# Filling empty expert slots row by row, one load for two heads' queries, and accumulating writes of one expert without dependence, in a fused attention and expert kernel

## The chip, the cores and the metric

One core of a Trainium2 chip runs the whole program. The metric is the device time of one launch in microseconds (us), the median of the runs. The engines are PE (TensorE, matrix products; its weight loads are counted apart as PEld), DVE (VectorE), ACT (ScalarE), POOL (GpSimd) and SP (SyncE), which does no arithmetic here and issues transfers. A "q" behind an engine's name (SPq, POOLq) is its sequencer, which issues transfers and waits. The core's transfers run on 16 DMA engines.

## The reference

Three layers follow each other.

1. Attention with a bucket mask, for 2 batches, 8 heads, 768 positions and a head width of 64. Each query and key gets six sign bits from a projection; a query sees only keys with the same bits. Softmax over the scaled scores, then the product with `v`.
2. A dense layer on the 1536 tokens of width 512: `h = x @ w_in` (512 to 2048), `g = h * sigmoid(1.702 h)`, `g @ w_out` (back to 512).
3. A mixture of 8 experts. Noisy gate logits pick two experts for each token:

```python
for e in range(E):
    for k in range(2):
        mask = top2[:, k] == e
        h = np.maximum(x[mask] @ w1[e], 0.0)
        out[mask] += top2_w[mask, k, None] * (h @ w2[e])
```

The operands of the products are split into a high and a low float16 half, and three products of halves replace one exact product.

## The kernel before

**Steps.** The work of layers 1 and 2 is laid out over numbered steps. A step `g` from 0 to 95 is one tile of 128 queries of one head against its 768 keys (`qk` L245, `rowmax` L258, `expo` L264, `e_hi` L301, `e_lo` L312 or, for the first 16, `e_turn` L278). Four such tiles (two heads by two tiles) make a unit, four units a chunk of 256 tokens, and there are six chunks. Some steps after a chunk's attention its dense layer follows in 16 pieces (`moe_pe` L446), then its routing (`route` L566). Tables in `PARAM` (L55, L56) say at which step each load, split and transpose stands.

**Order on the engines.** The program names each operation in the order of these steps. Up to step 99 a planner that comes with the language, which follows a modelled timeline, decides the order on each engine and its queue; from step 100 on (`GM=100`, L56, L950) the order is the one written out. The expert layer lies wholly in the written part.

**Loads.** All plain loads go through SP's queue. `load` (L115) fetches the queries of one unit in two transfers, one for each head of the pair (L120), into one tile `x`, and keys and values in one transfer for each head (L124). `stack_hi` (L128) and `stack_lo` (L151) split them; `stack_lo` also issues the first transpose of the stacked rows (L167, also on SP's queue), whose result `buckets` (L169) multiplies on PE (L177) to get the sign bits. `one_hot` and `stack_end` follow, with the second transpose (L209); then `qk` can use the unit. In the steps from 16 on the exponentials are also transposed by SP's queue (L323, tile `et`).

**Slots.** Tokens reach their experts through a table in DRAM, `slots`: rows of 1032 16-bit words (`ROW`, L30), of which 1024 are the token's two halves and 8 are token number, expert and weights. Expert `e` owns the 432 rows from `e * 432`. Not all are taken, so all 3456 are first filled by `init_slots` (L546), in seven calls at the steps 16, 18, ... 28. A call fills 512 rows (the last one 384): for each group of 128 rows one transfer writes the first 1024 words from a tile of zeros, 256 words at a time (L550), then one transfer writes the last 8 words of all groups from the tile `blank` (L552), where a row of its own behind the real output, `N + lane`, stands as the token number. The tiles `zeros`, `blank` and `blank2` are set on POOL at the start (L518 to L527). `init_out` (L554) fills the output with zeros, from the same tile `zeros`.

**Routing.** `r_t` (L561) transposes a tile of 128 tokens into a tile `xrt`, which has two buffers (the pool's default); `route` computes gate and position, and scatters the rows into `slots` with indirect transfers on POOL (L679). Before each one stands a memset of a one-element tile, `spacer` (L678), and the scatters are declared to have no dependence on each other (L683).

**Experts.** For each expert, `l1` (L785) and `l2` (L806) are the two products on PE. `l2` makes tiles 0 to 2 of 128 rows and a tile 3 of the last 48 rows, which is laid out as two halves of 256 columns. `l2_out` (L822) scales the tile on ACT (L828) and adds it to the output in DRAM with an accumulating indirect transfer on POOL (L830). All these adds go to one tensor with rows known at run time only, so each waits until the one before it has landed. Expert 0 is cut into two parts of two tiles each; the others have one part. The last expert's tile 3 is the last work of the program; behind it stands only a test whether any expert has over 432 tokens (L1033, L1034), which is false here.

Of the kernel before, what the change touches and what calls it, by code (L numbers as in the profile page):

```python
# [9 lines left out]
I32 = mybir.dt.int32  # L10
U32 = mybir.dt.uint32
I64 = mybir.dt.int64
U16 = mybir.dt.uint16
# [4 lines left out]
B, H, S, D = 2, 8, 768, 64  # L18
DM = H * D
N = B * S  # L20
# [9 lines left out]
ROW = 2 * DM + 8  # L30
NT = S // 128
HP = H // 2
CT = 2
# [21 lines left out]
PARAM = dict(GM=16, HE=lambda nm, b: 'D', OE=lambda nm, b: 'D', SC=lambda nm, b: 'D', WB=0, XO=lambda b: 'D', NG=16, WS=lambda i: 'P', TS=lambda g: True, XL=lambda g: 'D', GW=2, E0=7, T0=12, T1=16, EL=8, WX=3, PV={(1,2,3):4}, PVD=5, ST={}, VA={}, RA={}, O0=48, OS=2, IS=2, FU=16, VF=2, EC=lambda g: 'AA', QX=8, QS=3, EA=1, S1=(8,8,8,9,9,9,11,13), QE=8, XG=2, XB=2, PC=2, OH=3, BK=3, R0=18, R1=0, LK=8, WL=1, NW=3, LE=lambda nc: nc.scalar, I0=24, LQ=8, LV=0, W=[(g, 1) for g in range(-6, 30)], KA={(0,0,0):-8,(0,0,1):-6,(0,1,0):-4,(0,1,1):-2}, QA={(0,0,0):-7,(0,0,1):-3}, HI=lambda g: 'P', LO=lambda g: False)  # L55
# [4 lines left out]
def fused(ctx: ExitStack, tc: tile.TileContext, q, k, v, proj, w_in, w_out, w_gate, w_noise, noise,  # L60
          w1, w2, out, dbg=None):
    nc = tc.nc
    consts = ctx.enter_context(tc.tile_pool(name="consts", bufs=1))
    wts = ctx.enter_context(tc.tile_pool(name="wts", bufs=4))
    rt = ctx.enter_context(tc.tile_pool(name="rt", bufs=2))
# [14 lines left out]
                            channel_multiplier=1)  # L80
# [34 lines left out]
    def load(nm, b, u):  # L115
        hp, i = u
        if nm == "q":
            x = att.tile([128, 2, CT, D], F32, name="q32")
            for h in range(2):
                PARAM['LE'](nc).dma_start(x[:, h], q[b, 2 * hp + h].rearrange(  # L120
                    "(p c) d -> p c d", c=NT)[:, i * CT:(i + 1) * CT])
        else:
            x = att.tile([128, 1, NT, D], F32, name=f"{nm}32", tag="x32", bufs=4)
            PARAM['LE'](nc).dma_start(x[:, 0].rearrange("p c d -> p (c d)"), (k if nm == "k" else v)[b, 2 * hp + i].rearrange(  # L124
                "(p c) d -> p (c d)", c=NT))
        raw[nm, b, u] = x
# [366 lines left out]
    def moe_split(ci, i):  # L493
        if i < 8:
            th = mst.pop((ci, "th", i))
            if i % 2 == 0:
# [11 lines left out]
                            channel_multiplier=-1)  # L508
# [8 lines left out]
    nc.gpsimd.iota(tok, pattern=[[S, B], [1, NT]], base=0, channel_multiplier=NT)  # L517
    zeros = consts.tile([128, 256], U16)  # L518
    nc.gpsimd.memset(zeros, 0)
    blank = consts.tile([128, ROW - 2 * DM], U16)  # L520
    nc.gpsimd.memset(blank, 0)
    nc.gpsimd.iota(blank[:, :2].bitcast(I32), pattern=[[1, 1]], base=N, channel_multiplier=1)
    blank2 = consts.tile([128, ROW - 2 * DM], U16)
    nc.gpsimd.memset(blank2, 0)
    for h in range(2):
        nc.gpsimd.iota(blank2[h * 64:h * 64 + 64, :2].bitcast(I32), pattern=[[1, 1]], base=N + 128,
                       channel_multiplier=1)  # L527
# [16 lines left out]
    slots = dram.tile([E * N, ROW], U16)  # L544

    def init_slots(i):  # L546
        sl = slots[i * 512:min(i * 512 + 512, E * CAP)].rearrange("(k p) c -> p k c", p=128)
        n = sl.shape[1]
        for k_ in range(n):
            nc.sync.dma_start(sl[:, k_, :2 * DM].rearrange("p (u c) -> p u c", c=256),  # L550
                              zeros[:, None, :].to_broadcast([128, 2 * DM // 256, 256]))
        nc.sync.dma_start(sl[:, :, 2 * DM:], blank[:, None, :].to_broadcast([128, n, ROW - 2 * DM]))  # L552

    def init_out(i):  # L554
        n = min(NO - i * 128, 128)
# [156 lines left out]
    spacer = consts.tile([1, 1], F32)  # L712


    ew, eblk, xg, met, hts, yst = {}, {}, {}, {}, {}, {}

    def w12_load(e, i):
        x = m2.tile([128, 1024], F32, name="w32", bufs=4)
        eblk[e, i] = x
        if i < 4:  # L720
            nc.sync.dma_start(x, w1[e, i * 128:(i + 1) * 128, :])
        else:
            f = (i - 4) * 256
            nc.sync.dma_start(x.rearrange("p (a d) -> p a d", a=2),
                              w2[e, f:f + 256, :].rearrange("(a p) d -> p a d", p=128))
# [13 lines left out]
    def parts(e):  # L739
        return ((0, REG), (REG, CAP)) if e < EA else ((0, CAP),)  # L740
# [81 lines left out]
    def l2_out(e, p, t):  # L822
        wv, ti = met[e, p]
        o = t - parts(e)[p][0] // 128
        py = yst.pop((e, "y", t))
        nd = DM if t < NF else 256
        yo = m2.tile([128, DM], F32, name="yo", bufs=4)
        nc.scalar.activation(yo[:, :nd], py[:, :nd], AF.Copy, scale=wv[:, 0, o:o + 1])  # L828
        dst = out if t < NF else out.rearrange("n (a d) -> (n a) d", a=2)
        nc.gpsimd.indirect_dma_start(  # L830
            out=dst, out_offset=bass.IndirectOffsetOnAxis(ap=ti[:, o:o + 1], axis=0),
            in_=yo[:, :nd], in_offset=None, compute_op=OP.add)


    todo, first, early = {}, {}, {}
# [31 lines left out]
    def stacks(g, nm, b, u):  # L867
        oh = PARAM["OH"]
        at(g - 2, load, nm, b, u)
        at(g, stack_hi, nm, b, u)  # L870
        soon(g + 1, stack_lo, nm, b, u)
        start(g + PARAM['BK'], buckets, nm, b, u)
        at(g + oh, one_hot, nm, b, u)
        soon(g + oh + 1, stack_end, nm, b, u)

    for b in range(B):
        for hp in range(HP):
            g = b * NCH * 16 + 4 * hp
            for h in range(2):
                stacks(PARAM["KA"].get((b, hp, h), g - LK + 2 * h), "k", b, (hp, h))  # L880
                gv = next(x for x in range(g, NU, 16) if x >= FU) - PARAM["VA"].get((b, hp, h), LV - h)
                at(gv - 3, load, "v", b, (hp, h))
                soon(gv, v_hi, b, (hp, h))
                at(gv, v_lo, b, (hp, h))
            for cc in range(NCH):
                if g + 16 * cc < FU:
                    at(max(g + 16 * cc - PARAM["VF"], -2), v_load32, cc, hp)
        for cc in range(NCH):
            for hp in range(HP):
                g = (b * NCH + cc) * 16 + 4 * hp  # L890
                stacks(PARAM["QA"].get((b, cc, hp), g - LQ), "q", b, (hp, cc))
                gp = g + PARAM["PV"].get((b, cc, hp), PARAM["PVD"] if b * NCH + cc else 4)
                at(g + 3, norm, b, cc, hp)
                at(gp, pv, b, cc, hp)
                soon(gp + 1, pv_scale, b, cc, hp)
                at(gp + 1, pv_norm, b, cc, hp)
                at(gp + 2, pv_out, b, cc, hp)
# [17 lines left out]
    for i in range(-(-E * CAP // 512)):  # L915
        at(PARAM["I0"] + PARAM["IS"] * i, init_slots, i)
# [82 lines left out]
    for e in range(1, E):  # L999
# [5 lines left out]
        for i in range(8):  # L1005
            x = b0 + (b1 - b0) * i // 8 if e >= EA + 1 else PARAM["S1"][i]
# [11 lines left out]
    for x in range(-4, len(seq) + 2):  # L1018
        for _ in range(PARAM["QX"]):
            if x >= PARAM["QS"]:  # L1020
                next(gen, None)
        if 0 <= x - 1 < len(seq):
            k_, *a = seq[x - 1]
            (l1_out if k_ == "1" else l2_out)(*a)
        if 0 <= x < len(seq):
            k_, *a = seq[x]
            (l1 if k_ == "1" else l2)(*a)
        by_turns(todo.pop(x, []))
# [5 lines left out]
    with tc.If(most > CAP):  # L1034
        with tc.tile_pool(name="ov", bufs=1) as ov:
# [10 lines left out]
            x = ov.tile([128, 1024], F32)  # L1046
            wt = [wts.tile([128, 2, 4096], F16, name=f"wo{i}", tag="w") for i in range(2)]
            nc.vector.memset(cur, 0.0)
            with tc.For_i(0, E, 1) as e:
# [5 lines left out]
                with tc.If(here > CAP):  # L1055
                    for j, (src, sw) in enumerate(((w1, SW1), (w2, SW2))):
                        for i in range(4):
# [6 lines left out]
                            sl = slice(i * 1024, i * 1024 + 1024)  # L1064
# [76 lines left out]
```

## Time and profile before

| | us |
|---|---|
| runs | 850.34, 852.13, 854.86 |
| median | 852.13 |
| the profiled execution: its own time | 851.51 |
| the profiled execution: its span | 849.4 |

The profile shows one execution. Its span begins and ends with the first and the last record, and its own time is 2.1 us longer. Views used here: the page (busy time of each engine, and the span in 40 slices); the table by stretches; the timeline of an engine or queue, where the bracket behind a row tells how long the engine had been idle and what ended that; the list of waits (an engine and line, what released it, total, times, longest); the sums of one line; and the chain that ended last, in order of time. Rows of one kind may be merged, with their number behind an x.

### The profile page before, as it was taken

To read this page: it belongs to the slowest core of one execution; us is meant where nothing else is said; L and a number is where in the kernel's file an instruction comes from. 1 tells how busy PE (TensorE), PEld (TensorE's weight loads), DVE (VectorE), ACT (ScalarE), POOL (GpSimd) and SP (SyncE) were. 2 spreads that over 40 slices of the span, in tenths; PEclk is the share of its full clock that TensorE was granted. 3 is DMA by queue.
4 is the path that set the end of the run, shared out by engine and by line. 5 is a ranking of instruction groups with operands and counts; after the bars stand their busy time and mean duration, and the time that the engine had idled before them with its cause. 6 is when DMAs were issued, how large, how long until landed. Compare 5 with 4: busy or idle time off the path is not lost. (4 is left out here: it accounts for less than half of the span.)

```text
span 849.4 us, 14814 instructions
## 1 busy us (share of the span) xinstructions
PE 734.0 (86%) x5398; PEld 447.3 (53%) x5399; DVE 541.0 (64%) x1327; ACT 443.5 (52%) x859; POOL 270.9 (32%) x272
## 2 busy tenths in 40 slices
PE   1577658878988989798999999879999999999994
PEld 1354336435754665475567585556455554545542
DVE  8998679987896888568778527444543625335110
ACT  3777657657766686467467335244443434425210
POOL 6355437743334154214312143041021121211212
PEclk9988979998999999989999999989999999999997
DMA  8999998998999999976777634587865757766212
GB/s 205 227 253 230 210 223 179 220 212 173 179 155 214 161 190 194 223 134 106 149 131 122 139 108 122 177 200 167 221 145 168 209 120 194 156 172 162 38 15 36
DMA packets 285453, 141.03 MB, mean 166 GB/s; under 512 B 231552, under 2 KB 264384, under 8 KB 285376
## 3 DMA queue, kind: packets, MB, share of 16 engines
q1 hardware_dynamic: 278848, 126.37, 68.4%
q0 software_dynamic: 6528, 13.68, 9.2%
q8 instruction: 43, 0.70, 0.4%
q14 instruction: 34, 0.28, 0.1%
HBM read 61.49 MB, written 24.25 MB: 101 GB/s over the span
## 5 line engine op out<-in xcount | busy, mean ns | idle before, releaser
L792 PE MATMUL ph<-xg,ew 128*128 128x432 f16 (+2 forms) x864 | 146.8, 334 | 8.7 <-DMA xg<-slots 8.7
L456 PE MATMUL h<-xt,wi 128*128 128x256 f16 x1152 | 139.8, 276 | 2.0 <-DVE th L486 1.7
L467 PE MATMUL px<-wo,gt 128*128 128x512 f16 x576 | 134.9, 388 | 7.2 <-ACT wo L441 3.9
L736 DVE SCALAR_TENSOR_TENSOR ew<-w,ew 128x1024 f16<-128x1024 f32 x64 | 78.0, 1228 | 89.9 <-ACT ew L735 89.9
L830 POOL DMA_INDIRECT out_dram<-yo,ti x32 | 51.9, 1621 | 232.4 <-ACT yo L828 163.1
L814 PE MATMUL py<-ew,ht 128*128 128x512 f16 x576 | 125.8, 379 | 0.0
L456 PEld LDWEIGHTS <-wi 128*128 128x128 f16 x1152 | 112.1, 99 | 24.8 <-issue 5.5
L792 PEld LDWEIGHTS <-ew 128*128 128x128 f16 x864 | 85.3, 101 | 68.3 <-issue 6.4
L252 PE MATMUL s<-kt,qt 128*128 128x512 f16 (+1 forms) x384 | 90.6, 362 | 18.6 <-ACT e L271 14.6
L271 ACT ACTIVATE e<-s,mx 128x768 f32<-128x768 f32 x96 | 85.7, 894 | 34.0 <-DVE mx L262 19.7
L501 POOL TENSOR_TENSOR gt<-th,gt 128x512 f16<-128x512 f32 x48 | 60.2, 1254 | 114.9 <-ACT gt L500 111.3
L467 PEld LDWEIGHTS <-gt 128*128 128x128 f16 x576 | 55.9, 99 | 73.7 <-issue 10.6
L261 DVE TENSOR_REDUCE mx<-s 128x1 f32<-128x768 f32 x96 | 90.7, 949 | 6.3 <-PE s L252 6.1
L814 PEld LDWEIGHTS <-ht 128*128 128x128 f16 x576 | 56.3, 98 | 67.2
L319 DVE SCALAR_TENSOR_TENSOR er<-e,mx,er 128x768 f16<-128x768 f32 x68 | 71.2, 1049 | 24.3 <-ACT er L310 22.6
L310 ACT ACTIVATE er<-e,mx 128x768 f16<-128x768 f32 x68 | 63.3, 934 | 38.1 <-DMA et<-er 24.2
L802 ACT ACTIVATE ht<-ph 128x432 f16<-128x432 f32 (+2 forms) x72 | 35.3, 490 | 82.2 <-PE ph L792 82.2
L803 DVE SCALAR_TENSOR_TENSOR ht<-ph,ht 128x432 f16<-128x432 f32 (+2 forms) x72 | 40.0, 556 | 55.3 <-ACT ht L802 54.6
L828 ACT ACTIVATE yo<-py,wv 128x512 f32<-128x512 f32 (+1 forms) x32 | 20.3, 633 | 103.3 <-PE py L814 54.7
L735 ACT ACTIVATE ew<-w 128x1024 f16<-128x1024 f32 x64 | 66.3, 1047 | 2.5 <-DMA w<-in_moe_w_dram 2.5
L364 PE MATMUL pv<-et,vt 128*64 128x256 f16 x720 | 53.8, 283 | 13.9 <-DMA et<-er 13.9
L252 PEld LDWEIGHTS <-qt 128*128 128x128 f16 x384 | 37.1, 104 | 49.0 <-issue 26.5
(192 smaller groups left out, 930.0 us busy)
## 6 DMA issues: line engine op xcount, KB each, us to landing
w<-in_moe_w_dram SPq DMA_DIRECT2D x64, 512.0 KB
wraw<-in_moe_w_in_dram SPq DMA_DIRECT2D x16, 512.0 KB
wraw<-in_moe_w_out_dram SPq DMA_DIRECT2D x16, 512.0 KB
slots<-zeros SPq DMA_DIRECT2D x27, 256.0 KB
v<-in_v_dram SPq DMA_DIRECT2D x24, 192.0 KB
out_dram<-zeros SPq DMA_DIRECT2D x13, 256.0 KB
k<-in_k_dram SPq DMA_DIRECT2D x16, 192.0 KB
q<-in_q_dram SPq DMA_DIRECT2D x48, 64.0 KB
```

The costliest lines, as they stand in the source:

```text
L252: nc.tensor.matmul(ps[:, n0 * 128:n1 * 128], qt[:, s, h, t, :], kt[:, s, h, n0:n1, :].rearrange("p c t -> p (c t)"), start=(s == 0), stop= ...
L261: nc.vector.reduce_max(mx[:, 0:1], st[g]["ps"][:, :S], axis=AX.X)
L271: nc.scalar.activation(e32, st[g]["ps"][:, :S], AF.Exp, scale=0.125, bias=st[g]["mx"][:, 1:2], accum_out=sms[b, cc, hp][:, 2 * h + t:2 * h ...
L310: nc.scalar.activation(er[:, 0], st[g]["e"], AF.Copy, scale=r)
L319: nc.vector.scalar_tensor_tensor(er[:, 1], d["e"], d["mx"][:, 3:4], er[:, 0], op0=OP.mult, op1=OP.subtract)
L456: nc.tensor.matmul(ph[:, a, :], wi[ws][:, d, f0:f0 + 128], xt[:, d, xs, :], start=(d == 0 and ws == 0 and xs == 0), stop=(d == HP - 1 and ...
L467: nc.tensor.matmul(px, gts[ci, f // 2][:, gs, f % 2, t * 128:t * 128 + 128], wo[ws][:, f, :], start=(f == 0 and gs == 0 and ws == 0), stop ...
L501: nc.gpsimd.tensor_tensor(gt[:, 1], th, gt[:, 0], op=OP.subtract)
L735: nc.scalar.activation(hi, x, AF.Copy, scale=SW1 if j == 0 else SW2)
L736: nc.vector.scalar_tensor_tensor(lo, x, SW1 if j == 0 else SW2, hi, op0=OP.mult, op1=OP.subtract)
L792: nc.tensor.matmul(ph[:, :c1 - c0], w[:, ws, d * FE + f * 128:d * FE + f * 128 + 128], xg[e, p][:, xs * HP + d, :], start=(d == 0 and ws = ...
L814: nc.tensor.matmul(py, ht[:, f, hs, t * 128:t * 128 + 128], w[:, ws, f * DM:(f + 1) * DM], start=(i == 0), stop=(i == n - 1))
```

## The change

Three edits. `load` fetches the queries of both heads of a unit in one transfer; the pieces stay 512 bytes long (128 float32). `init_slots` fills its 512 rows in one transfer, with whole rows of 1032 words, from a tile `blank` that is now 1032 words wide and is taken from the buffers of `xrt`; `xrt` so becomes 16 bytes wider in each partition, and one of its two buffers holds `blank` until the last fill has read it. `l2_out` declares that the adds of one expert carry no dependence on each other (those of different experts still do), and puts a memset of `spacer` before each.

```diff
@@ load
             x = att.tile([128, 2, CT, D], F32, name="q32")
-            for h in range(2):
-                PARAM['LE'](nc).dma_start(x[:, h], q[b, 2 * hp + h].rearrange(
-                    "(p c) d -> p c d", c=NT)[:, i * CT:(i + 1) * CT])
+            PARAM['LE'](nc).dma_start(x.rearrange("p h c d -> p h (c d)"), q[b, 2 * hp:2 * hp + 2].rearrange(
+                "h (p c) d -> p h (c d)", c=NT)[:, :, i * CT * D:(i + 1) * CT * D])
@@ constants
-    blank = consts.tile([128, ROW - 2 * DM], U16)
+
+    blank = rt.tile([128, ROW], U16, name="blank", tag="xrt")
     nc.gpsimd.memset(blank, 0)
-    nc.gpsimd.iota(blank[:, :2].bitcast(I32), pattern=[[1, 1]], base=N, channel_multiplier=1)
+    nc.gpsimd.iota(blank[:, 2 * DM:2 * DM + 2].bitcast(I32), pattern=[[1, 1]], base=N, channel_multiplier=1)
@@ init_slots
         sl = slots[i * 512:min(i * 512 + 512, E * CAP)].rearrange("(k p) c -> p k c", p=128)
-        n = sl.shape[1]
-        for k_ in range(n):
-            nc.sync.dma_start(sl[:, k_, :2 * DM].rearrange("p (u c) -> p u c", c=256),
-                              zeros[:, None, :].to_broadcast([128, 2 * DM // 256, 256]))
-        nc.sync.dma_start(sl[:, :, 2 * DM:], blank[:, None, :].to_broadcast([128, n, ROW - 2 * DM]))
+        nc.sync.dma_start(sl, blank[:, None, :].to_broadcast([128, sl.shape[1], ROW]))
@@ l2_out
+    adds = {}
...
-        nc.gpsimd.indirect_dma_start(
+        nc.gpsimd.memset(spacer, 0.0)
+        ins = nc.gpsimd.indirect_dma_start(
             out=dst, out_offset=bass.IndirectOffsetOnAxis(ap=ti[:, o:o + 1], axis=0),
             in_=yo[:, :nd], in_offset=None, compute_op=OP.add)
+        for o_ in adds.setdefault(e, []):
+            tc.declare_no_dep(ins.ins, o_.ins, reason="a token is in an expert's slots once")
+        adds[e].append(ins)
```

## Rows read from the trace of the kernel before

**Rows 1.** The table by stretches: core, us, busy time and instructions of each engine.

```profile
core 0: us, PE busy (x) PEld busy (x) DVE busy (x) ACT busy (x) POOL busy (x), PEclk, DMA share, GB/s
60.00:112.00 52.00, 33.63 (x244) 19.81 (x243) 39.55 (x86) 36.73 (x86) 24.07 (x21) 0.87 1.17 225
112.00:200.00 88.00, 69.29 (x507) 42.23 (x507) 80.51 (x151) 59.28 (x115) 46.94 (x39) 0.91 1.00 206
340.00:480.00 140.00, 129.78 (x1049) 84.84 (x1049) 103.34 (x288) 82.41 (x164) 34.60 (x32) 0.96 0.77 142
540.00:818.00 278.00, 272.89 (x1715) 151.87 (x1714) 119.42 (x240) 106.12 (x161) 51.65 (x35) 0.98 0.64 157
```

**Rows 2.** The chain that ended last, its end: start us, us, what.

```profile
818.37 10.37 PE py L814 x48
...
828.82 0.70 ACT yo L828
829.52 0.66 issue
830.18 4.86 DMA out_dram<-yo,ti
...
835.79 4.90 DMA out_dram<-yo,ti
```

**Rows 3.** The end on POOL and ACT, two timelines: start us, us, engine, line, operation.

```profile
835.79 1.55 POOL L830 DMA_INDIRECT out_dram<-yo,ti  x1 [4.06 <-DMA out_dram<-yo,ti]
841.47 1.55 POOL L830 DMA_INDIRECT out_dram<-yo,ti  x1 [4.13 <-DMA out_dram<-yo,ti]
...
834.00 0.69 ACT L828 ACTIVATE yo<-py,wv 128x512 f32<-128x512 f32 x1 [4.49 <-PE py L814]
836.75 0.47 ACT L828 ACTIVATE yo<-py,wv 128x256 f32<-128x256 f32 x1 [2.06 <-PEq L1034]
```

**Rows 4.** Waits of PE between 60 and 125 us: total us, times, longest.

```profile
PE pb L177 <- DMA qt<-qsa: 10.3, 3, 4.8
PE pv L364 <- DMA et<-er: 3.6, 1, 3.6
```

**Rows 5.** Timeline of SP's queue around the longest wait for a query transpose.

```profile
96.46 4.44 SPq L550 DMA_DIRECT2D slots<-zeros  x3
100.94 0.55 SPq L552 DMA_DIRECT2D slots<-blank  x1
101.66 2.41 SPq L167 DMA_TRANSPOSE qt<-qsa  x1
```

**Rows 6.** Timeline of PE, the product after the longest of these waits.

```profile
109.97 0.19 PE L177 MATMUL pb<-pq,qt 128*128 128x12 f16 x1 [4.79 <-DMA qt<-qsa]
```

**Rows 7.** Timeline of POOL, scatters declared free of each other, with their spacers.

```profile
527.38 1.13 POOL L679 DMA_INDIRECT slots<-xr,si  x1 [0.21 <-issue]
528.51 0.09 POOL L678 MEMSET spacer<- 1x1 f32 x1
528.82 1.39 POOL L679 DMA_INDIRECT slots<-xr,si  x1 [0.21 <-issue]
```

**Rows 8.** The sums of L830: from issue to landing of the 32 adds.

```profile
DMA to landing us min/median/max: 3.9/5.3/7.4
```

**Rows 9.** Sums of lines on SP's queue (ns min/median/max, first, last); x19: before 112 us.

```profile
L550 SPq DMA_DIRECT2D slots<-zeros x27: 372/527/1847, 60.4 to 183.1; - x27
L550 SPq DMA_DIRECT2D slots<-zeros x19: 372/527/1847, 60.4 to 110.6; - x19
L552 SPq DMA_DIRECT2D slots<-blank x7: 373/554/1185, 75.9 to 184.1; - x7
L120 SPq DMA_DIRECT2D q<-in_q_dram x48: 358/430/1722, 1.3 to 393.2; - x48
```

**Rows 10.** The table by stretches: fills of 512-byte pieces (first three), then larger loads.

```profile
60.00:62.00 2.00, 2.00 (x29) 1.30 (x29) 2.00 (x10) 1.79 (x4) 0.00 (x0) 1.00 1.01 332
62.00:64.00 2.00, 2.00 (x21) 1.28 (x16) 2.00 (x7) 2.00 (x7) 1.95 (x2) 1.00 0.98 265
64.00:66.00 2.00, 2.00 (x15) 1.30 (x14) 2.00 (x5) 1.90 (x5) 1.51 (x1) 1.00 1.17 308
486.00:488.00 2.00, 2.00 (x13) 0.93 (x11) 0.49 (x4) 0.18 (x1) 0.00 (x0) 1.00 1.02 408
488.00:490.00 2.00, 2.00 (x12) 0.98 (x10) 0.73 (x5) 0.00 (x0) 0.89 (x1) 1.00 1.04 420
```

**Rows 11.** Timeline of POOL at the start of the program.

```profile
2.21 0.30 POOL L519 MEMSET zeros<- 128x256 uint16 x1
2.46 0.09 POOL L521 MEMSET blank<- 128x8 uint16 x1
3.86 0.92 POOL L143 TENSOR_TENSOR k<-k,ks 128x384 f32<-128x384 f32 x1 [0.48 <-DVE ks L142]
```

**Rows 12.** Timeline of SP's queue, transposes of `r_t` into the two buffers of `xrt`.

```profile
203.79 1.26 SPq L564 DMA_TRANSPOSE xrt<-xr  x1
211.15 1.63 SPq L564 DMA_TRANSPOSE xrt<-xr  x1
```

## The prediction

> **What bounds the kernel now.** I read the table by stretches first, since the program has stages with different limits. In the expert layer PE is busy 272.89 of 278 us [rows 1]: no transfer, and no instruction on POOL, sets the time there. In the stretch from 60 to 112 us nothing is full except the transfers: PE is busy 33.63 of 52 us, DVE 39.55, ACT 36.73, while the DMA share is 1.17 [rows 1]. From 112 to 200 us DVE is busy 80.51 of 88 us. From 340 to 480 us PE is busy 129.78 of 140 us. So a shorter transfer can buy time between 60 and 112 us, less after that, and nothing between 540 and 818 us.
>
> Then I read the end of the chain that ended last. Up to 828.8 us it is PE. After that come tile 1's activation, its add, and the whole of tile 2's add, 4.86 and 4.90 us, one behind the other [rows 2]. The two timelines say why: ACT has tile 3 ready at 836.75 + 0.47 = 837.22 us, but POOL issues its add at 841.47 us, released by a landing transfer [rows 3]. The last add waits 4.2 us for nothing but the order of the adds.
>
> Last I looked at what PE waits for between 60 and 125 us: three waits, 10.3 us in all, for the first transposes of queries, and one of 3.6 us for an `et` transpose [rows 4]. Ahead of the longest, 4.79 us up to 109.97 [rows 6], SP's queue spent 4.44 + 0.55 us on issuing slot fills [rows 5].
>
> Sums are made against the profiled execution's own time of 851.51 us. The median shown is 852.13 us, so 0.6 us is added at the end. A run-to-run difference of 0.5%, 4.3 us, is about what a measurement of this kernel can tell from no change.
>
> **The adds.** Removed is the wait of tile 3's add for tile 2's landing. Tile 2's add loses its wait too: its activation ends at 834.00 + 0.69 = 834.69, and between activation and issue lies 0.66 us where nothing else held it [rows 2], so it goes at about 835.35 instead of 835.79. POOL is then held for 1.55 us [rows 3], to 836.9, and a spacer and its gap take 0.09 + 0.21 us [rows 7], to 837.2. Tile 3 is ready at 837.22; with the 0.66 us it goes at 837.88, or, if the gap is only the scatters' 0.21 us, at 837.43. That is 3.6 to 4.0 us before 841.47. I take 3.7. What follows the last issue stays, unless two adds in flight slow each other: adds land 3.9 to 7.4 us after issue, median 5.3 [rows 8], and the two that stood alone took 4.9 [rows 2]. If the last one takes the median instead, 0.4 is lost; if it takes the longest, 2.5. So the edit is worth between 1.1 and 4.0 us. In front of the end the same edit moves adds of tiles 3 earlier, off PE's path. The 32 spacers cost 32 x 0.3 us spread over an engine that is busy 51.65 of 278 us [rows 1]; what hides them is PE's stretch for each tile, and without that cover only the last one would stand in the path, 0.3 us.
>
> **The fills, as instructions.** 27 + 7 issues become 7. At the medians, SP's queue spends 27 x 0.527 + 7 x 0.554 = 18.1 us on them and will spend 7 x 0.554 = 3.9 us if an issue costs what it did, or 7 x 1.847 = 12.9 us if a transfer four times as large is issued like the longest now [rows 9]. So 5 to 14 us of issuing go, between 60 and 185 us. I take the median, 14, as an issue shows no reason to grow.
>
> **The fills, as bytes.** The zeros are 27 x 128 x 2048 B = 7.08 MB. In the 6 us in which they lead, the DMA engines move 332, 265 and 308 GB/s, 302 on average; in a stretch of larger loads, 408 and 420 GB/s [rows 10]. Whole rows of 2064 B lie between the two. At 302 GB/s the fill holds the DMA engines for 23.4 us, at 414 for 17.1: a gain between 0 and 6.3 us, of which 19 of 27 transfers [rows 9], 4.4 us, fall before 112 us. The writes of the last 8 words vanish into the rows. I take 4 us in all.
>
> A rule speaks against this part. The Trainium skill, "DMA: Bandwidth & Descriptors", section "Specifications", puts the smallest transfer at line rate at 512 B, which the zeros already have; by it the bytes would take as long as before, and the sum would be some 2 us higher, 847.5. This trace disagrees as far as it goes: 302 against 414 GB/s, though with fills and loads in opposite directions.
>
> **The queries.** 24 of 48 issues go, 24 x 0.43 = 10.3 us of SP's queue between 1 and 393 us [rows 9]. Pieces and bytes stay, and the split waited for both heads before. By itself I cost it at nothing: where SP waits for data, a shorter issue gives only a longer wait. It helps between 60 and 112 us, and is in the next estimate.
>
> **What reaches the end of attention.** PE's 10.3 us of waits for query transposes [rows 4] are the part of the stretch that queue time can give back. Below nothing it cannot be shown to go (a rival has that); above it are 10.3 us. The relief before 112 us, 19/27 of the 4 us of bytes, 2.8, and most of the issuing, is nearer to half of the stall than to either end, so I take 5 of 10.3. After 112 us DVE is nearly full and `et` transposes begin, and some of an early start is waited away; I let 3.2 of the 5 us arrive at 480 us. That share is a choice, with bounds 0 and 1.
>
> **The wider blank.** A memset of 256 words takes 0.30 us and one of 8 words 0.09 [rows 11], so 1032 words take about 0.09 + 1024 x 0.21 / 248 = 0.96 us, 0.87 more. POOL idles 0.48 us before its first subtraction of keys [rows 11]; beyond that, 0.4 us falls on the start. If the planner sets it later it costs nothing; at most 0.9. I take 0.4. The borrowed buffer is free in time: the last fill is issued at 184.1 us [rows 9] and the transpose that needs the buffer comes second, at 211.15 us [rows 12].
>
> **Sum.** 851.51 - 3.7 - 3.2 + 0.4 = 845.0, and with 0.6 for the median 845.6 us; I say 845.5.
>
> **The rivals.**
>
> *The front is given back.* DVE's and PE's full stretches after 112 us [rows 1] take up what the fills free; only the adds count: 852.1 - 3.7 = 848.4 us, from 847 to 851. For it speaks that PE is at 93% from 340 to 480 us; against it, that DVE has 7.5 us to spare from 112 to 200 us, PE 18.7. Chance 0.27. The rule above would put the bytes' share of the front here.
>
> *The front gives more.* All 10.3 us return, with the 3.6 us wait of the first `et` transpose [rows 4], and arrive: 852.1 - 3.7 - 13.9 = 834.5 us. For it speaks that PE, DVE and ACT all idle in that stretch. Chance 0.14.
>
> *Slower: the big fill stands before a transpose.* A fill is now one block of 1.06 MB, 3.5 us at 302 GB/s, and nothing can be put between its parts as the planner does now. Where a block lands just ahead of a query transpose, PE waits as at 109.97, 4.8 us [rows 5, 6]. Seven such places cost 7 x 4.8 = 33.6 us in place of 10.3, 23.3 more, and with the adds' gain 872 us at the worst; half of them 3.5 x 4.8 - 10.3 = 6.5 more, and 855 us; five 13.7 more, and 862 us. Against it: today's parts already stand three and four together. It decides from four of seven on. Chance 0.14, at about 860.
>
> *The adds still wait.* If the declared freedom doesn't reach the waits, the end stays and only the front counts: 849.3 us. Against it, the scatters with the same declaration are issued 1.44 us apart, and what ended the idle time between them was no transfer [rows 7]. Chance 0.04.
>
> **How the numbers follow.** The forecast has 0.41, with a range of its own from 840 to 848. Faster by over 0.5% means below 847.9: nearly all of the forecast, the whole of the second rival, and a small part of the first, 0.40 + 0.14 + 0.07 = 0.61. Slower means above 856.4: most of the third, 0.10. The rest, 0.29, is no change. The range leaves out the far half of the second rival and the far part of the third: 836 to 856.
>
> **What would show it.** In the changed kernel's trace POOL should issue the last two adds about 2.5 us apart, with no wait on a landing, and the last within a microsecond of its activation; the span should end some 8 us after it, as now. L550 and L552 give way to one line with 7 issues. PE's waits for query transposes between 60 and 125 us should be about 5 us rather than 10.3, the DMA share there lower, and the first product of the expert layer's unbroken PE stretch should begin about 3 us earlier. The prediction is wrong if that start doesn't move or moves later, above all if `et` or query transposes stand behind single fills of over 3 us.

## The result and the profile after

The changed kernel takes 838.79 us (median of 4 runs, 837.42 to 844.27) against 852.35 us for the kernel before in the same runs: ratio 0.9846, 95% interval 0.9813 to 0.9878. That is 13.6 us less, where 845.5 us had been forecast, with a range of 836 to 856. The profiled execution took 838.56 us, its span is 836.9 us; before these were 851.51 and 849.4.

The end first. The timeline of POOL in the kernel after, from its tile 1 of the last expert on, and then ACT's scaling of tile 3:

```profile
820.81 1.56 POOL L828 DMA_INDIRECT out_dram<-yo,ti  x1 [3.58 <-ACT yo L825]
821.79 0.62 POOL L827 MEMSET spacer<- 1x1 f32 x1
825.99 1.56 POOL L828 DMA_INDIRECT out_dram<-yo,ti  x1 [3.58 <-ACT yo L825]
826.97 0.62 POOL L827 MEMSET spacer<- 1x1 f32 x1
828.52 1.56 POOL L828 DMA_INDIRECT out_dram<-yo,ti  x1 [0.93 <-ACT yo L825]
...
827.77 0.47 ACT L825 ACTIVATE yo<-py,wv 128x256 f32<-128x256 f32 x1 [2.06 <-PEq L1035]
```

The two last adds are issued 2.53 us apart, and what released each is its activation, not the landing of another add [rows 3]. From the last issue to the end of the span there are 8.4 us, against 7.9 before. The landing of the last add is not what takes longer: the sums of its line for this one add, in the kernel after and then in the kernel of the fills alone (below), where it flies alone, say

```profile
DMA to landing us min/median/max: 3.7/3.7/3.7
```

```profile
DMA to landing us min/median/max: 3.8/3.8/3.8
```

What the further 0.4 us are isn't shown. The same distance can be taken over the whole end, from the start of the last full products on PE (L814 before, L811 after) to the end of the span. Before they start at 818.37 us [rows 2], 31.0 us ahead of the end. The chain that ended last has for the kernel after:

```profile
809.40 10.37 PE py L811 x48
```

That is 27.5 us ahead of the end. So the end gave 3.5 us, and 818.37 - 809.40 = 9.0 us came from somewhere ahead of it.

Next the table by stretches, which answers to [rows 1]. Kernel after:

```profile
60.00:112.00 52.00, 34.80 (x239) 21.04 (x239) 34.36 (x82) 36.07 (x84) 22.61 (x23) 0.80 1.10 334
112.00:200.00 88.00, 69.51 (x504) 42.21 (x504) 86.07 (x156) 58.42 (x113) 49.34 (x40) 0.89 0.84 189
200.00:340.00 140.00, 128.58 (x1153) 87.84 (x1153) 121.22 (x357) 97.42 (x211) 54.80 (x52) 0.96 0.85 169
340.00:480.00 140.00, 132.68 (x1116) 87.78 (x1113) 103.04 (x294) 84.56 (x168) 34.08 (x30) 1.00 0.63 136
```

Between 60 and 112 us, where the forecast had put its gain, DVE does less than before (34.36 us against 39.55) although the DMA engines move 334 GB/s instead of 225. The surprise is lower down: from 340 to 480 us the DMA share (the column ahead of the GB/s) is 0.63 instead of 0.77, at nearly the same rate (136 against 142 GB/s). The fills were at no time in that stretch. Nearly the same bytes hold the DMA engines for less time.

The planner has also put things elsewhere. From SP's queue in the kernel after:

```profile
59.24 0.43 SPq L548 DMA_DIRECT2D slots<-blank  x1
...
79.87 7.78 SPq L208 DMA_TRANSPOSE kt<-ks  x2
...
88.33 0.42 SPq L548 DMA_DIRECT2D slots<-blank  x1
...
98.80 7.83 SPq L552 DMA_DIRECT2D out_dram<-zeros  x9
```

All seven fills are issued between 59 and 88 us, not 60 to 184 [rows 9]. The 14 transfers that zero the output follow at 91 to 108 us; in the kernel before they stood at 310 to 361 us, which the sums of the line in that kernel say:

```profile
L556 SPq DMA_DIRECT2D out_dram<-zeros x14: 565/910/1401, 309.7 to 361.0; - x14
```

Last, PE's waits between 60 and 125 us, as in [rows 4], kernel after:

```profile
PE s L251 <- ACT e L270: 7.8, 8, 2.7
PE s L251 <- DMA kt<-ks: 4.9, 1, 4.9
PE pv L347 <- DVE r L337: 2.7, 1, 2.7
PE pb L176 <- DMA qt<-qsa: 2.6, 1, 2.6
```

The waits for query transposes fell from 10.3 to 2.6 us, further than forecast, and bought nothing: a key transpose that is late takes 4.9 us, exponentials 7.8. Over all its lines the list has 22.2 us before and 22.5 after. The row maximum of step 12 (the thirteenth of its line on DVE) starts at 92.20 us, and at 76.67 us before: the early steps run later by up to 15 us.

### The profile page after: what moved, and what is told of

Read it like the earlier page. It is cut to its first block, busy times and chain, and to the rows that moved or that the text cites. A ratio compares the mean times of both kernels' runs of the same rounds, so it can differ in the third digit from the quotient of the medians.

```text
span 836.9 us, 14780 instructions
## 1 busy us (share of the span) xinstructions
PE 729.9 (87%) x5398; PEld 447.9 (54%) x5399; DVE 545.7 (65%) x1327; ACT 442.1 (53%) x859; POOL 272.4 (33%) x304
## 5 line engine op out<-in xcount | busy, mean ns | idle before, releaser
L455 PE MATMUL h<-xt,wi 128*128 128x256 f16 x1152 | 143.1, 280 | 4.3 <-DVE th L485 2.5
L811 PE MATMUL py<-ew,ht 128*128 128x512 f16 x576 | 125.8, 379 | 0.0
L251 PE MATMUL s<-kt,qt 128*128 128x512 f16 (+1 forms) x384 | 85.8, 345 | 34.3 <-ACT e L270 22.6
L466 PEld LDWEIGHTS <-gt 128*128 128x128 f16 x576 | 55.6, 99 | 70.0 <-issue 10.3
L811 PEld LDWEIGHTS <-ht 128*128 128x128 f16 x576 | 56.4, 98 | 67.2
L363 PE MATMUL pv<-et,vt 128*64 128x256 f16 x720 | 50.9, 280 | 0.9 <-DMA et<-er 0.9
```

The costliest lines, as they stand in the source:

```text
L251: nc.tensor.matmul(ps[:, n0 * 128:n1 * 128], qt[:, s, h, t, :], kt[:, s, h, n0:n1, :].rearrange("p c t -> p (c t)"), start=(s == 0), stop= ...
L455: nc.tensor.matmul(ph[:, a, :], wi[ws][:, d, f0:f0 + 128], xt[:, d, xs, :], start=(d == 0 and ws == 0 and xs == 0), stop=(d == HP - 1 and ...
L466: nc.tensor.matmul(px, gts[ci, f // 2][:, gs, f % 2, t * 128:t * 128 + 128], wo[ws][:, f, :], start=(f == 0 and gs == 0 and ws == 0), stop ...
L811: nc.tensor.matmul(py, ht[:, f, hs, t * 128:t * 128 + 128], w[:, ws, f * DM:(f + 1) * DM], start=(i == 0), stop=(i == n - 1))
```

## The experiments

Twelve kernels were run, each beside the kernel before on the same chip. Ratios are to that kernel, with 95% intervals. The theories were named A (fewer and longer pieces of the fills, as forecast), B (the zeroing of the output leaves the stretch from 310 to 360 us), C (another order by the planner, by luck) and, after the first four, D (the addresses of tiles). All of them compute the whole output.

### The adds alone

The kernel before with the third edit of the diff, as it stands there.

> The kernel before with the third edit alone: the adds of one expert free of each other, with spacers. My theory: the end of the program alone gets shorter, by 3.5 us as between the two traces (from the start of the last unbroken products on PE, L814, to the end of the span: 31.0 us before, 27.5 after); ratio 0.9959 (0.994 to 0.998). The start of the unbroken expert stretch on PE stays within 1 us of 567.1 us. Rival, that the freed adds also help or hurt earlier in the expert layer: that stretch's length (567.1 to 818.4, 251.3 us) changes by over 0.5 us, ratio below 0.993 or above 0.998.

Measured 847.59 us, 0.9925 (0.9901 to 0.9950). In its profile the last products start 27.25 us ahead of the end (820.25, span 847.5), so the end is shorter by 3.8 us, against 3.5 in the kernel after; the first unbroken products of an expert start 3 us later than before (570.07 against 567.08), not sooner. The runs show more, 4.3 us at the least by the interval. So the ratio missed its range and lies where the rival put it. The rival's other sign is there too, but weak: the unbroken stretch up to the last products is 1.1 us shorter (250.2 against 251.3 us), and in the kernel of the fills, where the adds still wait, it is 250.6. Where adds were put on top of another edit below, they took 3.3 and 2.7 us off (0.9827 against 0.9865, 0.9807 against 0.9839). I take some 3.5 us; why the adds alone gave more stays open.

### The fills alone, and the queries alone

The kernel before with the second edit, then with the first, as they stand in the diff.

> The kernel before with the second edit alone: slots filled in whole rows, seven transfers. The planner's order for this kernel puts the 14 zero fills of the output before 130 us, as in the kernel after, and not at 310 to 360 us. Theory A (the prediction's): fewer, longer pieces give back PE's waits before 125 us: steps 12 to 30 run 3 to 5 us earlier than before, ratio about 0.996. Theory B (the fills of the output leave the stretch from 310 to 360 us): steps 12 to 30 run later than before, as they do in the kernel after (by 8 to 15 us), and the gain comes between steps 63 and 78; ratio 0.988 to 0.992. Theory C (luck of the order): any ratio, with no gain at steps 63 to 78.

> The kernel before with the first edit alone: both heads' queries in one transfer. The planner's order for this kernel spreads the zero fills of the output from about 110 us to some 300 us. Theory A: nothing by itself, ratio 0.998 to 1.002. Theory B: with the output's fills mostly out of the stretch from 310 to 360 us, part of the gain comes at steps 63 to 78 although no byte is saved: ratio 0.990 to 0.996. Theory C: anything, with the difference elsewhere.

The fills gave 839.88 us, 0.9839 (0.9806 to 0.9873): by themselves as much as the whole change. In their profile step 12 starts 0.9 us earlier than before, step 21 0.6 us later and step 30 2.2 us earlier, less than A expected, and the steps 63 to 78 take 66.4 us instead of 79.9, which is where B put its gain. The queries gave 858.16 us, 1.0050 (1.0033 to 1.0066): a loss. In the kernel of the queries 12 of the 14 transfers that zero the output are issued before 280 us, and as B says, the later steps do run quicker. The row maxima of step 63 in the kernel before, then of the steps 63 and 93 with the queries:

```profile
326.69 0.95 DVE L261 TENSOR_REDUCE mx<-s 128x1 f32<-128x768 f32 x1
```

```profile
341.61 0.94 DVE L260 TENSOR_REDUCE mx<-s 128x1 f32<-128x768 f32 x1
...
466.16 0.95 DVE L260 TENSOR_REDUCE mx<-s 128x1 f32<-128x768 f32 x1
```

From step 63 to 93 it takes 124.6 us; the kernel before takes 133.2 (its step 93 starts at 459.88). But it comes to step 63 already 14.9 us late, so it is still 6.3 us late at step 93. Whether the moved zeroing gave the 8.6 us between, or a late kernel catches up there, isn't shown. The lateness can be followed on SP's queue of that kernel:

```profile
70.79 2.53 SPq L549 DMA_DIRECT2D slots<-zeros  x4
...
78.89 4.71 SPq L208 DMA_TRANSPOSE kt<-ks  x2
```

The last two key transposes of the first batch are issued at 79 us, behind fills and value loads; before they were issued at 69 and 73 us. Step 12 starts at 87.17 us in place of 76.67. The kernel after has the same lateness (its L208 at 79.87), the kernel of the fills has not (step 12 at 75.8, counted in the same way). So in both kernels with the merged load the planner's order is worse at this place. That this order is the whole of the loss was not tried by itself.

The fills' profile shows the same drop of the DMA share as the kernel after, and the one of the queries doesn't. From 340 to 480 us, the fills and then the queries:

```profile
340.00:480.00 140.00, 134.12 (x1118) 88.86 (x1115) 101.78 (x289) 82.09 (x162) 35.16 (x30) 0.99 0.62 135
```

```profile
340.00:480.00 140.00, 133.16 (x1097) 88.44 (x1096) 106.11 (x295) 89.95 (x177) 39.89 (x37) 0.98 0.75 136
```

### The output zeroed late

```diff
# in the kernel after
-    nc.gpsimd.memset(zeros, 0)
@@ init_out
+        if i == 0:
+            e = st[PARAM["O0"] + 1]["e"]
+            nc.gpsimd.tensor_tensor(zeros.bitcast(F32), e[:, :128], e[:, :128], op=OP.subtract)
```

> The kernel after, all three edits, with the output's zero tile made on GpSimd from data of step 57 (a tile minus itself), so that none of the 14 zero fills of the output can be issued before about 300 us, as in the kernel before. Theory A: the gain stays, ratio to the kernel before 0.984 to 0.987, since whole-row fills and merged queries give it. Theory B: the gain between steps 63 and 78 goes, some 8 us, ratio 0.992 to 0.997, and the early steps run sooner than in the kernel after. Theory C: neither; the order of all engines is another again, and the gain appears or goes elsewhere.

Measured 842.52 us, 0.9856 (0.9825 to 0.9886), well inside the interval of the kernel after. As the whole cause B falls: the output is zeroed late again (307.9 to 346.6 us) and the gain stays. A share of a few us is not excluded: in the profiles the steps 63 to 93 take 128.3 us here and 122.9 in the kernel after. The gain that stays was also the outcome A asked for, but A has no reason for the DMA share of 0.62 to 0.63 far behind the fills in the kernels of the fills and after (here it is 0.70, with zeroing up to 347 us in that stretch). What fills, kernel after and this kernel have in common is `blank` in the buffers of `xrt`. It takes 32 bytes per partition out of the constants and makes the two buffers wider, and every tile behind them gets another address. By the program's own allocation (bytes in a partition; in brackets the remainder by 256):

```
                                    before          after
er (source of the et transposes)    209632 (224)    209664 (0)
                                    212704 (224)    212736 (0)
et (their destination)              191200 (224)    191232 (0)
kt, qt                              153472 (128)    153504 (160)
```

### Nothing but a pad

An unused tile of 32 bytes, ahead of `e32`, `et` and `er`, or ahead of `er` alone. The instructions and their order on SP, PE and DVE are those of the kernel before.

```diff
# first pad: in expo
+        if g == 0:
+            att.tile([128, 1], F32, name="pad", bufs=1)
         e32 = att.tile([128, S], F32, name="e32")
# second pad: in v_load32, whose tile is the first with tag "er"
+        if cc == hp == 0:
+            att.tile([128, 1], F32, name="pad", bufs=1)
         x = att.tile([128, 2, NT, D], F32, name="v32", tag="er")
```

> The kernel before with one unused tile of 32 bytes in each partition ahead of the tiles e32, et and er, and nothing else: the order on SP, PE and DVE is the same instruction by instruction. It moves er (what the et transposes read) from addresses 224 bytes past a multiple of 256 to multiples of 256, and et (what they write) likewise, as the kernel after does by its 16-byte-wider buffers. Theory D (the address): the DMA share falls from 0.97 to about 0.86 between 200 and 340 us and from 0.77 to about 0.65 between 340 and 480 us, and the ratio is 0.985 to 0.994. Theory C (the planner's other order gave the gain) and theory A (fewer pieces of the fills): no change, ratio 0.998 to 1.002, DMA shares as before.

> As the run with the pad ahead of e32, but the pad lies behind et and ahead of er: only er, the source of the et transposes, moves to multiples of 256 bytes; et, their destination, stays 224 past. Theory D with the source deciding: as that run, ratio 0.985 to 0.994. Theory D with the destination deciding: no change, 0.998 to 1.002. Theories A and C: no change.

Both gave 0.9865 (0.9840 to 0.9889, and 0.9834 to 0.9897), 842.11 and 840.89 us: 11 to 12 us, for no change to any instruction but its addresses. Of what these transposes read and write the second moves the source alone, and it is enough; where the destination lies makes no difference. (Four kinds of tiles that don't take part in a transpose, `v32`, `r2`, `xn` and `vt`, move by 32 bytes with it.) The stretches of the second:

```profile
200.00:340.00 140.00, 130.47 (x1166) 87.44 (x1166) 117.52 (x357) 97.58 (x212) 57.64 (x55) 0.98 0.94 194
340.00:480.00 140.00, 132.51 (x1081) 86.80 (x1080) 103.65 (x288) 81.68 (x163) 35.42 (x32) 0.98 0.67 145
```

From 340 to 480 us the share is 0.67 against 0.77 [rows 1], while the rate rose from 142 to 145 GB/s, so it isn't that less was moved. (Up to 340 us the share was forecast at 0.86 and came out at 0.94: the rate rose there too, from 181 to 194.) PE's waits for these transposes between 200 and 480 us, kernel before, then the second pad:

```profile
PE pv L364 <- DMA et<-er: 9.0, 7, 4.3
```

```profile
PE pv L366 <- DMA et<-er: 4.2, 4, 2.3
```

And the row maxima on DVE show where the time is won. In the kernel before, then with the second pad, those of the steps 12, 21 and 93:

```profile
76.67 0.95 DVE L261 TENSOR_REDUCE mx<-s 128x1 f32<-128x768 f32 x1
...
115.52 0.94 DVE L261 TENSOR_REDUCE mx<-s 128x1 f32<-128x768 f32 x1
...
459.88 0.96 DVE L261 TENSOR_REDUCE mx<-s 128x1 f32<-128x768 f32 x1
```

```profile
76.87 0.94 DVE L263 TENSOR_REDUCE mx<-s 128x1 f32<-128x768 f32 x1
...
115.75 0.94 DVE L263 TENSOR_REDUCE mx<-s 128x1 f32<-128x768 f32 x1
...
448.90 0.96 DVE L263 TENSOR_REDUCE mx<-s 128x1 f32<-128x768 f32 x1
```

Up to step 21 the two agree within 0.3 us, since the first `et` transpose is issued at 111 us. From there to step 93 eleven microseconds are won, though single profiles of equally slow kernels can differ by four of them (see "Which multiple").

### The pad against the change

In the kernel after, a pad ahead of nearly all tiles, which puts `er` 32 bytes past a multiple of 256; and the fills alone with the same pad.

```diff
+    consts.tile([128, 1], F32, name="pad")
     ident = consts.tile([128, 128], F16)
```

> The kernel after with 32 unused bytes ahead of nearly all tiles, same order on SP, PE and DVE: er and et go to 32 bytes past a multiple of 256, the rest of the change stays. Theory D: about half of the gain or more goes, ratio to the kernel before 0.990 to 0.996 (the adds alone gave 0.9925 with an interval of 0.990 to 0.995), and the DMA share between 340 and 480 us rises from 0.63 to about 0.75. Theories A and C: the ratio stays at 0.983 to 0.987.

> The whole-row fills alone, as the run of the fills, with 32 unused bytes ahead of nearly all tiles: the order on SP, PE and DVE is that run's, but er starts 32 bytes past a multiple of 256 again, not on it. This leaves what the fills do by their pieces, their issues and the planner's new order. Theory D: most of the fills' 1.6 per cent goes, ratio to the kernel before 0.994 to 0.999 (0.9839 of the fills over 0.9865 of the pad alone is 0.9974). Theory A and C: the gain stays, 0.981 to 0.988.

The kernel after fell back to 845.95 us, 0.9910 (0.9883 to 0.9936), with the DMA share from 340 to 480 us up from 0.63 to 0.72; step 93 starts 5 us later (457.9 against 452.87). So 0.64% of its 1.54% was the address; this pad moves nearly all tiles, so that it is the address of `er` follows from the other pads and not from this run. The fills alone fell back to 842.86 us, 0.9917 (0.9896 to 0.9938), half of their gain. The gain that stays, 0.8%, is more than D expected (a ratio of 0.994 to 0.999). The single profile of this run is its fastest execution (839.38 us of 839.38 to 845.66), with a span like that of the unpadded fills, so the difference between these two is one of the medians. In the two profiles step 93 starts at 450.76 without and at 451.06 with the pad, although the sums of the `et` transposes, first without and then with it, show them slower:

```profile
DMA to landing us min/median/max: 3.2/3.4/7.1
```

```profile
DMA to landing us min/median/max: 3.7/4.0/7.8
```

So how the address costs time in this order is not shown. Whether the remaining 0.8% comes from longer pieces, from fewer issues or from the order was not separated. With the pad, too, the steps 63 to 78 take 65.3 us instead of 79.9, the place that B named, so the moved zeroing stays a candidate for it.

### More tiles on multiples of 256

```diff
# in the kernel after, expo: sm moves from pool att to pool rt
-            sm = att.tile([128, 4], F32, name="sm", bufs=3)
+            sm = rt.tile([128, 4], F32, name="sm", bufs=3)
```

> The kernel after with the 96 bytes of the small tile sm taken from another pool, same order on SP, PE and DVE: er and et stay on multiples of 256 bytes, and the sources and destinations of the query and key transposes (qsa, qsb, ks, qt, kt), of the experts' token transposes (xg) and the weight and query loads come to multiples of 256 as well (they lie 96 to 160 past now). Theory D: the DMA share falls once more, most between 0 and 200 us, and the time by 2 to 6 us against the kernel after; ratio to the kernel before 0.977 to 0.983. Theories A and C: as the kernel after, 0.983 to 0.987.

A miss: 839.10 us, 0.9851 (0.9817 to 0.9885), no better than the kernel after; the share from 340 to 480 us is 0.65, not lower. Where the 32 key and 48 query transposes start, and where the 9 token transposes write (they read from DRAM), doesn't set the time. These transposes hardly got faster either: at the median the first ones of queries and keys (L166) landed after 3.3 us instead of 3.5, the second ones (L208) after 3.3 instead of 3.2.

### Which multiple

The pad ahead of `er` with 96 bytes in place of 32.

> The kernel before with a pad of 96 bytes ahead of er in place of 32: er starts 64 bytes past a multiple of 256, a multiple of 64 but not of 256; same order on SP, PE and DVE. If the pieces of 256 bytes that the transposes read must start on a multiple of 256: slow as before, ratio 0.997 to 1.003, DMA share 0.75 to 0.78 between 340 and 480 us. If a multiple of 64 is enough: 0.984 to 0.990 and 0.66 to 0.69, as with the pad of 32.

```profile
340.00:480.00 140.00, 130.75 (x1087) 86.02 (x1084) 102.04 (x281) 80.79 (x162) 33.78 (x31) 0.98 0.74 141
```

849.62 us, 0.9992 (0.9976 to 1.0008): 64 past a multiple of 256 is as slow as 224 past. On the multiple itself it is 0.9865. The time from issue to landing of the 80 `et` transposes says the same more directly than the share. With 64 past, then on the multiple (the second pad):

```profile
DMA to landing us min/median/max: 3.6/4.1/7.7
```

```profile
DMA to landing us min/median/max: 3.2/3.6/8.0
```

All kernels follow this, whatever their order (the trace of the kernel before has no landing times): the five with `er` off a multiple that have them (adds, queries, 64 past, and the two with the pad of 32 ahead of nearly all tiles) have a least time of 3.6 to 3.7 us and medians of 4.0 to 4.1, the eight with `er` on it 3.2 us and 3.4 to 3.6.

One profile is less sharp. With 64 past, a kernel as slow as the one before, step 93 starts at

```profile
455.99 0.96 DVE L263 TENSOR_REDUCE mx<-s 128x1 f32<-128x768 f32 x1
```

and 3.9 us later in the kernel before. So the ratios, and not a step of one profile, say what the address is worth.

### The parts put together

The fills with the adds, without the queries; and the pad ahead of `er` with the adds, without either of the other edits.

> The kernel after without the merged query load: whole-row fills and freed adds. If the parts add up, 0.9839 for the fills less 3.5 us (0.0041) for the end: ratio 0.978 to 0.982, 834 to 838 us, some 3 us below the kernel after, since the queries alone made the kernel 0.5 per cent slower. If the queries' loss was the planner's order in that one kernel and no property of the edit: as the kernel after, 0.983 to 0.987.

> The kernel before with the freed adds and the 32-byte pad ahead of er, and none of the two other edits: the fills of 512-byte pieces and the two query loads stay. If the address and the end are all that pays, 0.9865 less 0.0041: ratio 0.980 to 0.984, as good as the kernel after or better. If fills and queries give a further part of the gain of the kernel after: 0.986 or above is not expected by either; a result between 0.984 and 0.986 would say that the end is worth less here.

The first gave 833.88 us, 0.9807 (0.9785 to 0.9829), the second 836.27 us, 0.9827 (0.9808 to 0.9846). Both lie below the kernel after (0.9846). The first has the lowest ratio of all; without the merged load of the queries the change is worth about 0.4% more, near the 0.5% which that load cost alone, and the intervals of the two overlap a little. A pad of 32 bytes and the freed adds, eight new lines, do at least as well as the whole change.

## Why the prediction was right or wrong, point by point

**Sign and range** came true: faster, and 838.8 us lies in 836 to 856. The likeliest case's own range, 840 to 848, was missed, and the forecast gain of 6.6 us is half of the 13.6 measured. That the range was met is in part luck: some 5.5 us of the gain came from tile addresses, which no term of the sum had.

**The adds** went as worked out: forecast 3.7 us, between 1.1 and 4.0; 3.5 measured in the traces. The last issue comes 4.0 us sooner, the top of the range (19.1 us after the start of the last products instead of 23.1), and 0.45 us are lost behind it (8.4 us instead of 7.9). The loss is about as large as the one allowed for, but not for that reason: the last add landed 3.7 us after its issue, as fast as alone.

**What reaches the end of attention** was the step that failed. It was put at 3.2 us, from PE's waits for query transposes ahead of 125 us; 9.0 us arrived. Even its first half was wrong: those waits did fall, but other waits took their place and the early steps ran up to 15 us later, so nothing was handed on from there. The larger part of what did arrive, some 5.5 of the 9.0 us by the kernel after with the pad (0.9910 against 0.9846), goes with the addresses, above all with the source of the 80 `et` transposes behind 111 us, which moved onto a multiple of 256 bytes. The rest came with the fills and the queries; whether by bytes, issues or the planner's order (and in it the place of the output's zeroing) stays open. The change's words held it (a buffer 16 bytes wider), and the working used them only to see that the borrowed buffer is free in time. The addresses of the tiles behind it were not followed. With the address taken out, fills, queries and adds together leave 0.9910, 7.7 us: close to the 6.6 forecast, but by a different split (a loss of the queries of 0.4 to 0.5%, forecast at nothing, against a larger gain of the fills).

A rule of the Trainium skill offers a reason. "DMA: Bandwidth & Descriptors", section "How a descriptor splits into AXI transactions", says that a transaction must start at a multiple of 256 bytes, so that a piece which starts between two of them begins with a transaction of which only a part is used. By an estimate from that page a 256-byte piece would need two transactions instead of one. The runs agree as far as they go: 0.9865 at a multiple, 0.9992 at 64 past one, and at the median 3.6 and 4.1 us from issue to landing. They show neither the transactions themselves nor the size of the pieces. The rule is about any descriptor; here the destination's place made no difference, and the page's section "DMA Transpose (X-bar)" asks for 32 bytes only, which every tile here had all along.

**The fills as instructions**: 7 issues with a median of 0.489 us, forecast 0.554; none grew beyond 1.77. Right for the kernel after (with the fills alone the median is 0.879), but SP's queue was not relieved, since the planner put 14 other transfers into the room. That the planner would fill the room was in none of the steps.

**The fills as bytes**: 4 us were taken, between 302 and 414 GB/s. In the kernel after, where most of the fills are on their way:

```profile
70.00:84.00 14.00, 9.47 (x72) 5.65 (x70) 9.33 (x19) 9.64 (x24) 7.04 (x9) 0.87 1.07 371
```

At 371 GB/s, a rate with other transfers in it as the 302 was, 7.08 MB take 19.1 us instead of 23.4, so the size was right for the engines. What it was worth in program time was not measured by itself. With `er` off its multiple all that the fills do gives 0.8%, some 7 us.

**The queries**, costed at nothing, cost about 4 us; the likely way is the planner's later order of the key transposes, which was not tried alone.

**The wider blank**: the memset took 0.95 us, forecast 0.96. POOL's first subtraction of keys starts at 4.00 us instead of 3.86, 0.14 us later in place of 0.4, because the planner set three small operations (L522 and L526) behind it.

**The rivals.** "The front gives more" had nearly the right time for the wrong reason. "The big fill stands before a transpose" did happen, in part: key transposes stood behind fills, step 12 was 15 us late, and had caught up by step 36, at 206 us in both kernels. But with the queries alone they stood behind small fills as well, and with the big fills alone step 12 was not late, so the size of the fill was not what did it.

## What to carry to other kernels

When a tile is added, dropped or widened, look at where the tiles behind it come to lie, above all the sources of DMA transposes: a start on a multiple of 256 bytes was worth 11 us of 852 in the kernel before and some 5.5 in the kernel after, and a pad of 32 bytes bought it. An edit that goes through a planner should be compared by the order that comes out, transfers it doesn't touch included, and a pad or an edit that leaves the order unchanged is the clean experiment. Where writes can't meet, freeing them from each other pays at the end of the program, where nothing covers the wait (3.5 us here).

## What the runs showed of the hardware

The 80 DMA transposes of a [128, 1536] float16 tile in SBUF to another tile there depend on where their source starts. With remainders by 256 bytes of 32, 64 and 224 they landed at the earliest 3.6 to 3.7 us after issue, at the median after 4.0 to 4.1; with remainder 0 at the earliest after 3.2 us, at the median after 3.4 to 3.6. The DMA share from 340 to 480 us was 0.72 to 0.77 with the former and 0.62 to 0.70 with the latter, at 134 to 145 GB/s throughout. The destination's remainder of 224 or 0 made no difference (0.9865 both). For the smaller query and key transposes, moved from a remainder of 160 to 0, no gain was seen.
